# A kernel ordered by a planner: durations and port use in the list of steps corrected, and the first sums of w1 moved to the first part

## The chip, the cores and the metric

The kernel runs on one core of a Trainium2 chip. The metric is the device time of one execution in microseconds (us), median over several runs. The engines are named as in the profile: PE (TensorE, matmuls and transposes), ACT (ScalarE), DVE (VectorE), POOL (GpSimd) and SP (SyncE, which issues most of the transfers).

## The reference

Two blocks follow each other; all results are float32.

```
# block 1: attention with positive random features; q, k, v: (8, 8, 576, 64), omega: (128, 64)
x_s  = x / 64**0.25                                   # for q and k
h    = x_s @ omega.T - sum(x_s*x_s)/2
phi  = exp(h - max(h)) / sqrt(128)
kv   = phi(k).T @ v ;  z = sum over positions of phi(k)
x    = (phi(q) @ kv) / (phi(q) @ z + 1e-6)            # heads joined: (8, 576, 512)
# block 2: Fourier mixing and a multi-layer perceptron
u    = x + real(fft(fft(x, axis=1), axis=2))
un   = (u - mean(u)) / sqrt(var(u) + 1e-6)
out  = u + maximum(un @ w_ch1, 0) @ w_ch2             # w_ch1: (512, 2048), w_ch2: (2048, 512)
```

## The kernel before

**Two parts.** The first part works through 32 pairs of heads, 8 batches of 4 pairs. It also mixes each batch when its four pairs are there, converts both weight matrices from 64-bit to 32-bit floats, and puts the first four tiles of 128 rows ("plain" blocks) through the perceptron by plain products. The second part puts the other 4096 rows through it in eight blocks of 512 rows (`TB`), with products of half size in a Strassen-like scheme: sums of quarters of the weights and of the activations are formed on DVE and POOL, and fewer products are left for PE.

**A pair of heads** takes these steps (lines of the kernel before): transposes of k and q (`tps`, L396), evicted by ACT (`kqT`, L403); products with omega (`pp`, L471 for two heads at a time in quarters of the array, L461 for the odd column); maxima on DVE (`nmx`, L412) and exponentials on ACT (`e`, L424); the product with v (`kvp`, L506), kept by DVE or ACT (`kv`, L521 or L523); transposes of the query features (`tps`, L396); and the last products (`ndp`, L550 and L558), which DVE divides and writes to the batch's frame `x` (L571 to L581). L581 writes three times for each pair, and it is the pair's last step.

**Mixing a batch**: DVE, or for one half POOL, folds the frame (L608 to L636), PE multiplies by tables of cosines and sines (`yp`, L654; `ab`, L681 and L686), ACT and DVE combine the results (L700 to L708), and DVE and POOL add them to the frame (L716, L717), which SP stores to DRAM (`us`).

**Converting the weights**: 32 slabs of 128 x 512 numbers, 16 of w1 and 16 of w2, are loaded through POOL's queue (L358). For each slab, in the function `narrow`: L331 on POOL or L333 on ACT scales the upper words; L335, L337, L340 and L342 on DVE move bits; L344 on POOL adds. Only after all 32 slabs may `w2_parts` (L956) form sums of w2, which go to DRAM, and only then may the rows of the first block of the second part be normalised into the same slabs.

**A plain block**: normalised rows (L792 to L806) give `hp` (L863, 16 x 4 products), the relu `ht` is taken by ACT or DVE (L849, L847), and `op` (L886, 16 products of 512 columns) adds up the result, to which DVE adds the residual (L899).

**The second part**: `first_of` (products L1059, sums L1121 on POOL, relu sums L1047 on DVE, saves L1073 on ACT) and `product_of` (products L1204, sums L1174 on DVE, additions to the result L1243 on POOL or DVE). Before its first products, `weight_sums` forms four groups of sums of w1 on DVE (L1044): each group is four instructions of 128 x 512, for two of the eight columns of `first_of`. They lie in `w1s`, a buffer that is allocated when the buffers of the first part are freed, as `hid`, `hs` and the saves `s` are.

**What sets the order.** Every engine works through its instructions in the order in which they were issued. That order comes from a planner in the kernel (`Listing`): each stream yields steps (`Step`) with an engine or a choice of engines, a duration in us, what it waits for, what buffers it takes and gives, and a bias. The planner keeps a time at which each engine is free, and issues again and again the step that could start first, where the bias is added to the start for the comparison alone. The planned durations are thus not measured at run time; they only decide the order, and for steps with a choice the engine. `port=True` marks a step that uses the SBUF port which DVE and POOL share: the planner does not let two of these overlap. The central lines of its function `start`:

```
        if step.port:
            t = max(t, self.free[PORT])
        eng = min(step.engines, key=lambda e: max(t, self.free[e]) + step.engines[e])
```

Of the kernel before, what the change touches and what calls it, by code (L numbers as in the profile page):

```python
# [35 lines left out]
PORT = "port"  # L36
# [24 lines left out]

class Fork:
# [4 lines left out]
class Listing:  # L67
# [11 lines left out]
    def start(self, step, ready, before):  # L79
# [13 lines left out]
        if step.port:  # L93
            t = max(t, self.free[PORT])
        eng = min(step.engines, key=lambda e: max(t, self.free[e]) + step.engines[e])
        t = max(t, self.free[eng] if eng != NONE else 0.0)
        return t + (TURN if eng == PE and step.mode != self.mode else 0.0), eng

    def run(self, streams):
# [16 lines left out]
        while todo:  # L116
# [17 lines left out]
            if step.port:  # L134
                self.free[PORT] = end
# [46 lines left out]
def kernel(  # L182
# [38 lines left out]
    NWL, NSUM = 15, 3  # L221
# [37 lines left out]
    def loads():  # L259
        for n in range(B * NP):  # L260
# [7 lines left out]
            yield Step(SP, 0.45, 3.6, makes=("kq", n), kb=288)  # L268
            nc.sync.dma_start(kq[:, R : 2 * R, :], q[b, h].rearrange(rows, r=R))
            if n == 0:  # L270
                yield from load_v(0)

    def load_v(n):
        b, pr = divmod(n, NP)
        yield Step(SP, 0.6, 4.0, take=(f"vd{n % NV}",), makes=("vd", n), kb=288)
        nc.sync.dma_start(
            vds[n % NV][:, :, 0:D],
            v[b, 2 * pr : 2 * pr + 2].rearrange("i (p r) d -> (i p) r d", r=R),
        )

    def loads_v():
        for n in range(1, B * NP):
            yield from load_v(n)
# [25 lines left out]
    def load_tables():  # L309
        yield Step(NONE, after=(("kq", 2),))  # L310
        for n, a in tabs.items():
            yield Step(SP, 1.0, 4.0, makes=n, kb=a.nbytes / 1024)
# [8 lines left out]
    def narrow(i, dst, raw):  # L321
# [6 lines left out]
        step = Step({ACT: 0.7, POOL: 1.0}, after=(("raw", i),), bias=0.22)  # L328
# [5 lines left out]
        yield Step(DVE, 0.45, bias=0.02)  # L334
# [8 lines left out]
        yield Step(POOL, 1.3, makes=("w", i), give=("slab",), port=True, bias=0.12)  # L343
        nc.gpsimd.tensor_tensor(out=dst, in0=dst, in1=lof, op=ALU.add)  # L344

    def weights():
# [13 lines left out]
        yield Step(NONE, after=tuple(("w", i) for i in range(len(parts))), makes="converted", bias=1.84)  # L360
# [7 lines left out]
    def first():  # L368

        yield Step(NONE, 3.0, bias=-0.86)  # L370
# [29 lines left out]
    def evicted(dst, ps, j0, j1, makes, back):  # L400
        yield Step(ACT, 0.15 + 0.115 * (j1 - j0), 0.1, makes=makes + (j0,), give=("bank",), bias=0.03)
# [5 lines left out]
    def softmax(n, t, num, ps, es):  # L407
# [12 lines left out]
            ACT, 0.12 + 0.265 * num, 0.0, take=("e" if num == 4 else "e1",), give=("bank",), makes=("e", n, t), bias=0.17  # L420
# [11 lines left out]
    def attn(n):  # L432
# [16 lines left out]
        def pairs_of(js, *ts):  # L449
# [3 lines left out]
                0.45 if len(ts) == 1 else 1.0,  # L453
# [35 lines left out]
        def feature(c):  # L489
# [6 lines left out]
            1.35,  # L496
# [18 lines left out]
        def keep():  # L515
# [22 lines left out]
            1.3,  # L538
# [24 lines left out]
        yield Step(DVE, 1.6, after=(("frame", b),), give=("bank", "bank"), makes=("x", b, pr), bias=-0.06)  # L563
# [24 lines left out]
    def frames():  # L588
        for b in range(B):
            yield Step(NONE, take=(f"x{b % 2}",), makes=("frame", b), bias=0.16)  # L590


    def mix(b):
# [7 lines left out]
        def folds(n):  # L601
# [7 lines left out]
            step = Step({DVE: 1.15, POOL: 2.5} if n else DVE, 1.15, port=True)  # L609
            yield step  # L610
            eng = nc.gpsimd if step.eng == POOL else nc.vector
            eng.tensor_copy(
                out=h[:, NL, 0 : 2 * QD + 1 : 2 * QD], in_=x[:, 4, 0 : 2 * QD + 1 : 2 * QD]
            )
            for dst, src in ((h[:, 0:NL], h[:, 0:NL]), (h[:, NL : NL + 1], x[:, 4:5])):
                eng.tensor_tensor(
# [78 lines left out]
    def residual(b, c, x, ab):  # L695
        np_ = P if c < NL else 64
        yield Step(ACT, 0.4, 0.1, take=("bmp",), give=("bank",), bias=-0.02)
# [14 lines left out]
        def summed(g, left, right, which, dur):  # L712
            yield Step(which, dur, port=True, bias=-0.37)
# [6 lines left out]
            yield Step(SP, 0.4, 2.5, makes=("us", b, c, g), kb=2 * np_, bias=-1.96)  # L720
# [6 lines left out]
        yield Fork(summed(0, mi, pl, DVE, 0.8))  # L727
        if c < NL:
            yield from summed(1, pl, mi, POOL, 1.4)
        yield Step(NONE, after=(("us", b, c, 0),), give=("bmp",), bias=-1.98)  # L730
        if c == NL:
# [8 lines left out]
                kb=512,  # L740
# [42 lines left out]
    def norm_of(j, t, i, pool, dst):  # L783

        yield Step(SP, 0.5, 3.0, take=("u",), kb=256, bias=0.14)
# [5 lines left out]
        yield Step(DVE, 1.09, bias=0.16)  # L791
# [3 lines left out]
        yield Step(POOL, 0.6, port=True, bias=-0.1)  # L795
        nc.gpsimd.tensor_tensor(rstd[:], rstd[:], mhalf[:], op=ALU.pow)  # L796
        yield Step(DVE, 0.56, bias=-0.15)
# [7 lines left out]
        yield Step(ACT, 0.6, 0.1, give=("bank",), makes=("unT", j, i), bias=-0.27)  # L805
# [9 lines left out]
    def plain_norms():  # L815
        for j in range(NPLAIN):
            key = ("plain", j)
            yield Step(NONE, after=events_of([j]), take=("unT",), bias=0.34)
# [5 lines left out]
    def plain():  # L824
        for j in range(NPLAIN):
            if j == NPLAIN - 1:

                yield Step(NONE, after=(("x", B - 1, NP - 1),), bias=-0.24)
            yield from plain_of(j)

    def plain_of(j):
# [20 lines left out]
        for fc in range(NFC):  # L852
# [6 lines left out]
                give=("unT",) if fc == NFC - 1 else (), bias=0.19,  # L859
# [11 lines left out]
        for i in range(nt):  # L871
            for f0 in range(0, NFC, 2):
# [7 lines left out]
                    makes=("op", nt * j + i) if f0 == NFC - 2 else None, bias=0.18,  # L880
# [13 lines left out]
    def rest(t, yp):  # L894
        yield Step(SP, 0.5, 2.7, take=("ur",), kb=256, bias=1.91)
        ur = mlpp.tile([P, DM], F32, name="ur", tag="ur", bufs=1)
        load_rows(ur[:], t)
        yield Step(DVE, 0.7, after=(("op", t),), give=("bank",), bias=0.51)
# [38 lines left out]
    def w2_parts():  # L937
# [14 lines left out]
        def op(o, l, r, **kw):  # L952
            step = Step({DVE: 0.7, POOL: 1.35}, port=True, **kw, bias=0.39)
# [6 lines left out]
        for i, made_of in (  # L960
# [16 lines left out]
            yield Step(SP, 2.2, 4.5, after=(("w2t", i),), kb=7 * 256, makes=("w2l", i), bias=0.69)  # L977
# [7 lines left out]
        yield Step(NONE, after=last, give=("slab",) * 4, bias=1.32)  # L985
# [6 lines left out]
    def pairs(start):  # L992
# [11 lines left out]
        + [w2_parts(), block_norms(0, mlpp), plain(), weights()]  # L1004
# [16 lines left out]
    w1s = late.tile([128, 3, NDC // 2, DFF // 2], F32, name="w1s")  # L1021
    hid = late.tile([128, NFC, TB], F32, name="hid")
    hs = late.tile([128, HF, 3, HT], F32, name="hs")

    def sums_left(a11, a12, a21, a22, s1, s2, s4):

        return (
            (s1, a21, a22, ALU.add),
            (s2, s1, a11, ALU.subtract),
            (a21, a11, a21, ALU.subtract),  # L1030
            (s4, a12, s2, ALU.subtract),
        )

    def weight_sums():
        for g in range(4):
            f = slice(F2 // 4 * g, F2 // 4 * (g + 1))
            f2 = slice(F2 + f.start, F2 + f.stop)
            ops = sums_left(
# [298 lines left out]
```

## Time and profile before

| | us |
|---|---|
| median of 8 runs | 1237.85 (1237.3 to 1238.85) |
| the profiled execution, its own time | 1237.75 |
| its span from first to last instruction | 1236.0 |
| PE busy in the span | 1200.0 (97%) |
| DVE busy | 771.8 (62%) |
| ACT busy | 457.5 (37%) |
| POOL busy | 395.3 (32%) |
| first product of the second part starts at | 474.98 |

PE's busy time has modelled ends and includes products that run on a quarter of the array, so a busy PE isn't a PE at its peak. The granted clock of TensorE over the span is 0.996. In the groups of the profile the columns are: line, engine, operation, output and inputs with their shapes, count, then busy us, mean ns of one, and the idle time of the engine just before, with what ended it.

### The profile page before, as it was taken

Reading aid. Unit: us, or ns where it says so; the run is one execution under the profiler, and the core shown is the slowest. Engines: PE = TensorE matmul, PEld = TensorE weight load, DVE = VectorE, ACT = ScalarE, POOL = GpSimd, SP = SyncE. Lnnn points to the kernel's source line nnn. Section 1 sums busy time; section 2 is a strip of 40 time slices with the busy share of each in tenths; the row PEclk is TensorE's granted clock in tenths of the full one; section 3 lists DMA queues with packets and bytes.
Section 4 is the critical chain, followed back from the end, with each engine's and each line's share of the span. In section 5 each row is a group of like instructions: output and inputs, shape, how many; then the busy total and the mean of one; then the engine's idle time right before and its main releaser. Section 6 shows DMA issues by size and latency. Waiting matters only on the chain.

```text
span 1236.0 us, 31364 instructions
## 1 busy us (share of the span) xinstructions
PE 1200.0 (97%) x12513; PEld 1070.8 (87%) x12513; DVE 771.8 (62%) x1708; ACT 457.5 (37%) x1430; POOL 395.3 (32%) x462
## 2 busy tenths in 40 slices
PE   6999899999999998999999999999999999999997
PEld 5787778778887876899899899899899899899897
DVE  3999899997687525185185185186276276266265
ACT  5776666677664211222222222222222222222211
POOL 2544354643233110430430530530530530531430
PEclk8999999999999999999999999999999999999999
DMA  8655456646564345087078078078078068068155
GB/s 241 171 171 171 151 151 188 207 120 200 160 205 134 112 141 171 9 264 248 9 255 256 10 244 265 10 234 276 4 226 278 18 215 276 30 196 287 38 164 161
DMA packets 148737, 206.00 MB, mean 167 GB/s; under 512 B 49264, under 2 KB 62320, under 8 KB 148592
## 3 DMA queue, kind: packets, MB, share of 16 engines
q1 hardware_dynamic: 143984, 187.22, 48.2%
q0 software_dynamic: 4608, 16.78, 4.3%
q8 instruction: 100, 1.64, 0.5%
q14 instruction: 45, 0.37, 0.1%
HBM read 172.23 MB, written 35.91 MB: 168 GB/s over the span
## 4 chain that ended last, share of the span: by engine, by line
PE 83%; DVE 10%; ACT 3%; issue 2%; DMA 1%; SPq 0%; DVEq 0%; ACTq 0%
PE sx L1059 17%; PE sx L1204 16%; PE sz L1059 9%; PE sz L1204 8%; PE sy L1059 4%; PE hp L863 4%; PE sy L1204 4%; PE op L886 4%; PE tps L396 3%; PE yp L654 3%; PE pp L471 3%; ACT e L424 2%; DVE nmx L412 2%; PE kvp L506 1%; PE ndp L550 1%
## 5 line engine op out<-in xcount | busy, mean ns | idle before, releaser
L424 ACT ACTIVATE e<-pp,nmx 128x128 f32<-128x128 f32 x576 | 159.6, 407 | 47.2 <-DVE nmx L412 46.9
L1121 POOL TENSOR_TENSOR hs<-hid 128x256 f32<-128x256 f32 x64 | 46.6, 728 | 357.8 <-DVE hid L1047 330.2
L1047 DVE CUSTOM_DVE_ANT_0 hid<-sz,s 128x256 f32<-128x256 f32 x64 | 27.2, 425 | 182.4 <-PE sz L1059 174.4
L1059 PE MATMUL sx<-unT,w 128*128 128x256 f32 x512 | 127.7, 379 | 2.2 <-ACT s L1073 1.4
L1204 PE MATMUL sx<-wl,sums 128*128 128x128 f32 x896 | 115.4, 275 | 0.0
L1204 PE MATMUL sz<-wl,sums 128*128 128x128 f32 x896 | 114.2, 275 | 0.0
L412 DVE TENSOR_REDUCE nmx<-pp 128x4 f32<-128x512 f32 (+1 forms) x160 | 94.1, 628 | 31.1 <-PE pp L471 16.3
L1059 PEld LDWEIGHTS sx<-unT,w 128*128 128x128 f32 x512 | 96.6, 190 | 16.2 <-ACT s L1073 1.8
L1204 PEld LDWEIGHTS sz<-wl,sums 128*128 128x128 f32 x896 | 107.7, 192 | 0.4
L1204 PEld LDWEIGHTS sx<-wl,sums 128*128 128x128 f32 x896 | 107.6, 192 | 0.0
L1073 ACT ACTIVATE s<-sx 128x256 f32<-128x256 f32 x128 | 49.1, 384 | 152.1 <-PE sx L1059 74.2
L344 POOL TENSOR_TENSOR w<-w,raw 128x512 f32<-128x512 f32 x32 | 45.8, 1433 | 118.2 <-DVE raw L342 111.1
L1106 ACT ACTIVATE hid<-sx 128x256 f32<-128x256 f32 x64 | 24.6, 384 | 132.8 <-PE sx L1059 132.8
L471 PE MATMUL pp<-om,kqT 64*64 64x128 f32 x2048 | 71.1, 279 | 0.5 <-issue 0.3
L796 POOL TENSOR_TENSOR rstd<-rstd,mhalf 128x1 f32<-128x1 f32 x36 | 25.3, 704 | 142.8 <-DVE rstd L794 125.0
L471 PEld LDWEIGHTS pp<-om,kqT 64*64 64x64 f32 x2048 | 58.2, 136 | 11.9 <-issue 6.8
L1204 PE MATMUL sx<-wl,hid 128*128 128x128 f32 x512 | 67.6, 275 | 0.0
L863 PE MATMUL hp<-unT,w 128*128 128x128 f32 x512 | 62.2, 276 | 3.9 <-ACT e L424 2.9
L863 PEld LDWEIGHTS hp<-unT,w 128*128 128x128 f32 x512 | 59.5, 192 | 6.3 <-ACT e L424 3.5
L1059 PE MATMUL sx<-tt,w 128*128 128x256 f32 x256 | 64.2, 379 | 0.0
L1182 ACT ACTIVATE s<-sx 128x128 f32<-128x128 f32 x112 | 31.1, 278 | 88.5 <-PE sx L1204 60.7
L1059 PE MATMUL sz<-tt,w1s 128*128 128x256 f32 x256 | 61.9, 379 | 1.7 <-DVE w1s L1044 1.7
(134 smaller groups left out, 2578.6 us busy)
## 6 DMA issues: line engine op xcount, KB each, us to landing
wl<-w2l SPq DMA_DIRECT2D x392, 256.0 KB, 3.8
raw<-in_moe_w_ch_dram POOLq DMA_DIRECT2D x32, 512.0 KB, 4.8
kq<-in_k_dram SPq DMA_DIRECT2D x32, 288.0 KB, 3.6
kq<-in_q_dram SPq DMA_DIRECT2D x32, 288.0 KB, 5.0
vd<-in_v_dram SPq DMA_DIRECT2D x32, 288.0 KB, 4.7
out_dram<-ur SPq DMA_DIRECT2D x72, 128.0 KB, 3.0
u<-us SPq DMA_DIRECT2D x32, 256.0 KB, 4.5
ur<-us SPq DMA_DIRECT2D x32, 256.0 KB, 3.3
```

Of the source, the lines that this page charges most:

```text
L344: nc.gpsimd.tensor_tensor(out=dst, in0=dst, in1=lof, op=ALU.add)
L396: nc.tensor.transpose(ps[:, (j - j0) * 128 : (j - j0 + 1) * 128], src(j), ident[:])
L412: nc.vector.tensor_reduce(nmx[:, 0:num], ps[:, 0 : MF * num].rearrange("p (c m) -> p c m", m=MF), axis=AX.X, op=ALU.max, negate=True,)
L424: nc.scalar.activation(out=e[:, c, :], in_=ps[:, MF * c : MF * c + MF], func=AF.Exp, bias=nmx[:, c : c + 1],)
L471: nc.tensor.matmul(pps[c][cols, MF * m : MF * m + MF], lhsT=kqT[rows, j, cols], rhs=om2[rows, c, :],)
L654: nc.tensor.matmul(yp[:, 0:NK], lhsT=fold[:, c, n, :], rhs=tab[:, c, :], start=(c == 0), stop=(c == NC3 - 1),)
L863: nc.tensor.matmul(hp[:, 0:TP], lhsT=w1[:, dc, 128 * fc : 128 * fc + 128], rhs=unTs[key][:, dc, :], start=(dc == 0), stop=(dc == NDC - 1),)
L886: nc.tensor.matmul(yp[:, 0:DM], lhsT=hs[fc][:, 128 * i : 128 * i + 128], rhs=w2[:, fc, :], start=(fc == 0), stop=(fc == NFC - 1),)
L1059: nc.tensor.matmul(ps[:, 0:HT], lhsT=left(dc), rhs=right(dc), start=start and dc == 0, stop=(dc == D2 - 1), skip_group_check=True,)
L1073: nc.scalar.activation(out=s[:], in_=ps[:, 0:HT], func=AF.Copy)
L1121: nc.gpsimd.tensor_tensor(out=o, in0=l, in1=r, op=op)
L1204: nc.tensor.matmul(ps[:, 0:128], lhsT=left[:, f], rhs=wls[j, i, n][:, f], start=start and f == 0, stop=(f == 3), skip_group_check=True,)
```

## The change

These things are changed:

- The port is asked of the step and the engine: a step with `port=True` that goes to ACT no longer counts as using it, and one with a choice is planned with the port's time only for DVE and POOL.
- More steps are marked with `port`: L331 on POOL, L335, and the normalisation L798.
- Durations are set anew, as 1.4 instead of 1.0 us for L331 on POOL, 0.94 for `pp`, 1.1 for `kvp`, 1.23 for `ndp`, 0.85 and 1.6 for the sums L716 and L717; and many biases are set anew.
- The v of the first pair is a load of its own stream, no longer tied behind the first keys and queries; `kb` of a v load is set to 500.
- The second step of the second fold is always on DVE.
- The sums of the first of the four groups of w1 are made in the first part, after the last conversion, in a buffer `w1s0` of their own that lasts through both parts. The third sum of that group, which before overwrote a quarter of w1, goes to that buffer too, since plain blocks still read w1. `NWL`, the number of buffers for the loads of w2's parts, goes from 15 to 14.

```diff
+    def on_port(self, eng):
+        return self.port and eng in (DVE, POOL)
...
-        if step.port:
-            t = max(t, self.free[PORT])
-        eng = min(step.engines, key=lambda e: max(t, self.free[e]) + step.engines[e])
-        t = max(t, self.free[eng] if eng != NONE else 0.0)
+        def begin(e):
+            return max(t, self.free[e] if e != NONE else 0.0, self.free[PORT] if step.on_port(e) else 0.0)
+
+        eng = min(step.engines, key=lambda e: begin(e) + step.engines[e])
+        t = begin(eng)
...
-            if step.port:
+            if step.on_port(eng):
                 self.free[PORT] = end
...
-    NWL, NSUM = 15, 3
+    NWL, NSUM = 14, 3
...
             nc.sync.dma_start(kq[:, R : 2 * R, :], q[b, h].rearrange(rows, r=R))
-            if n == 0:
-                yield from load_v(0)
...
-        yield Step(SP, 0.6, 4.0, take=(f"vd{n % NV}",), makes=("vd", n), kb=288)
+        yield Step(SP, 0.6, 4.0, take=(f"vd{n % NV}",), makes=("vd", n), kb=500)
...
-            yield Step(SP, 1.0, 4.0, makes=n, kb=a.nbytes / 1024)
+            yield Step(SP, 1.0, 4.0, makes=n, kb=a.nbytes / 1024, bias=1.85)
...
-        step = Step({ACT: 0.7, POOL: 1.0}, after=(("raw", i),), bias=0.22)
+        step = Step({ACT: 0.72, POOL: 1.4}, after=(("raw", i),), port=True)
...
-        yield Step(DVE, 0.45, bias=0.02)
+        yield Step(DVE, 0.43, port=True)
         nc.vector.tensor_scalar(hi, hi, 0x80000000, None, op0=ALU.bitwise_and)
...
-        yield Step(ACT, 0.15 + 0.115 * (j1 - j0), 0.1, makes=makes + (j0,), give=("bank",), bias=0.03)
+        yield Step(ACT, 0.15 + 0.115 * (j1 - j0), 0.1, makes=makes + (j0,), give=("bank",), bias=-1.56)
...
-                0.45 if len(ts) == 1 else 1.0,
+                0.44 if len(ts) == 1 else 0.94,
...
-            1.35,
+            1.1,
             mode="quarters",
...
-            1.3,
+            1.23,
             mode="halves",
...
-            step = Step({DVE: 1.15, POOL: 2.5} if n else DVE, 1.15, port=True)
-            yield step
-            eng = nc.gpsimd if step.eng == POOL else nc.vector
-            eng.tensor_copy(
+            yield Step(DVE, 1.15, port=True)
+            nc.vector.tensor_copy(
...
-        yield Step(POOL, 0.6, port=True, bias=-0.1)
+        yield Step(POOL, 0.7, port=True, bias=0.23)
         nc.gpsimd.tensor_tensor(rstd[:], rstd[:], mhalf[:], op=ALU.pow)
-        yield Step(DVE, 0.56, bias=-0.15)
+        yield Step(DVE, 0.56, port=True)
...
+    GW = F2 // 4
+    w1s = [const.tile([128, 4, D2, GW], F32, name="w1s0")]
+
+    def weight_sums(groups):
+        yield Step(NONE, after=("converted",))
+        for g in groups:
...
+                if g == 0 and i == 2:
+                    o = w1s[0][:, 3]
+                nc.vector.tensor_tensor(out=o, in0=l, in1=r, op=op)
...
-        + [w2_parts(), block_norms(0, mlpp), plain(), weights()]
+        + [w2_parts(), weight_sums((0,)), block_norms(0, mlpp), plain(), weights()]
...
-    w1s = late.tile([128, 3, NDC // 2, DFF // 2], F32, name="w1s")
+    w1s += [late.tile([128, 3, D2, GW], F32, name=f"w1s{g}") for g in range(1, 4)]
...
-        product(x, lambda d: w1[:, d, f2], lambda d: un[1][:, d], False)
+        product(
+            x,
+            lambda d: w1s[0][:, 3, d, fg] if g == 0 else w1[:, d, f2],
+            lambda d: un[1][:, d],
+            False,
+        )
...
-    listing.run([late_norms(), halves(), loads_w2(), weight_sums()])
+    listing.run([late_norms(), halves(), loads_w2(), weight_sums((1, 2, 3))])
```

## The prediction

> **What bounds the kernel now.** I read the page first, then the busy time by stage, then the groups by form, then the timeline at two places. The page, parts 1 and 2:
>
> ```profile
> PE 1200.0 (97%) x12513; PEld 1070.8 (87%) x12513; DVE 771.8 (62%) x1708; ACT 457.5 (37%) x1430; POOL 395.3 (32%) x462
> PE   6999899999999998999999999999999999999997
> DVE  3999899997687525185185185186276276266265
> ```
>
> TensorE looks full throughout, but VectorE is full only in slices 2 to 9, and a PE that is "busy" on 64-wide products can be slow. The busy time by stage (columns: stretch, its length, then PE, PEld, DVE, ACT, POOL, each with its count, granted clock, DMA share, GB/s):
>
> ```profile
> 0.00:40.00 40.00, 29.66 (x604) 24.09 (x607) 19.46 (x40) 25.07 (x82) 12.39 (x23) 0.91 0.78 226
> 40.00:257.00 217.00, 205.06 (x3946) 172.01 (x3945) 206.56 (x490) 149.94 (x500) 103.80 (x94) 1.00 0.58 174
> 257.00:400.00 143.00, 140.01 (x2519) 118.05 (x2517) 112.79 (x295) 90.87 (x298) 44.08 (x38) 1.00 0.52 163
> 400.00:474.00 74.00, 74.00 (x417) 53.64 (x416) 30.60 (x72) 14.45 (x44) 8.01 (x10) 1.00 0.32 106
> 474.00:490.00 16.00, 12.10 (x54) 9.91 (x54) 11.86 (x20) 3.30 (x9) 0.34 (x1) 1.00 0.77 257
> 490.00:584.00 94.00, 94.00 (x633) 88.12 (x633) 49.78 (x102) 22.46 (x64) 29.28 (x39) 1.00 0.56 179
> ```
>
> From 40 to 257 us DVE is 95% busy (206.56 of 217) and sets the pace; from 257 on DVE has gaps and PE sets it; a block of the second part (490 to 584) is PE at 94.0 of 94.0. So time can come only from 0 to 490.
>
> What DVE does in its full stage, from the groups by form (columns: count, busy us, mean ns, idle before):
>
> ```profile
> L335 DVE TENSOR_SCALAR raw<-raw 128x512 uint32<-128x512 uint32 x32 | 21.8, 699 | 0.0
> L337 DVE SCALAR_TENSOR_TENSOR w<-w,raw 128x512 uint32<-128x512 uint32 x32 | 27.6, 863 | 0.3
> L340 DVE TENSOR_SCALAR raw<-w 128x512 uint32<-128x512 uint32 x32 | 19.8, 620 | 1.1
> L331 POOL TENSOR_SCALAR w<-raw 128x512 f32<-128x512 f32 x27 | 44.9, 1670 | 27.0 <-DMA raw<-in_moe_w_ch_dram 26.8
> L333 ACT ACTIVATE w<-raw 128x512 f32<-128x512 f32 x5 | 3.6, 711 | 1.1 <-DMA raw<-in_moe_w_ch_dram 1.1
> ```
>
> The view of line 335 alone gives the spread, min/median/max:
>
> ```profile
> L335 DVE TENSOR_SCALAR raw<-raw x32: 409/421/1584, 30.0 to 264.7; 128x512 uint32<-128x512 uint32 x32
> ```
>
> Half of these take 421 ns, some up to 1584: the excess is about the length of a POOL instruction. The same views give medians 682 for L337 and 430 for L340. A conversion thus loses (699-421)+(863-682)+(620-430) = 0.65 us of DVE to collisions with POOL.
>
> Two places of the timeline fix the clock of the argument. The twentieth of the 32 attention pairs ends here (L581 writes its result), and the second part begins so:
>
> ```profile
> 255.53 0.94 DVE L581 TENSOR_TENSOR x<-ndp,rden 128x256 f32<-128x256 f32 x3
> 474.98 1.96 PE L1059 MATMUL sx<-unT,w 128*128 128x256 f32 x8 [0.87 <-DVE ur L899]
> 477.82 0.69 DVE L1044 TENSOR_TENSOR w1s<-w 128x512 f32<-128x512 f32 x1 [2.98 <-DMA out_dram<-ur]
> 478.61 1.97 PE L1059 MATMUL sz<-tt,w1s 128*128 128x256 f32 x8 [1.67 <-DVE w1s L1044]
> ```
>
> **The change, part by part.** The list decides order and engine, so I compared the instruction orders of both programs, which are fixed when they are built.
>
> *To the twentieth pair.* At the lowest duration of each group, the DVE rows up to there add to 230.0 us before and 229.3 after: no work leaves DVE. What can leave is the collisions. Through pair 20 the old list has 28 conversions: 28 x 0.65 = 18.2 us; with the small copies L612 (8 x 0.17), the sums L716 and L717 (8 x 0.20 and 8 x 0.30 over their lowest) and L608 and L798 (0.5), 24 us. In the new order line 331 runs 15 times on POOL (26 before, through that pair) and the rest on ACT. If collisions go with that count, 42% of 24 go: 10 us. All of them at most: 24. L331, L335 and L798 are now kept off the port by the list, which before counted none of the three, so more than the count should go. I take 15, nearer to the end that a count supports; the lower bound is 0, if real times drift from the planned ones. Pair 20 then ends at 256.5-15 = 241.5.
>
> A rule that speaks against this: by the Trainium skill, GPSIMD Engine Reference, Engine selection, a one-input operation runs on GpSimd at roughly line rate; its elementwise section has 1.03 cycles per element, an estimated 0.44 us for 512, so moving 11 of them would free 4.8 us of port and the gain would be nearly nil. The row says 1670 ns, so I go by 11 x 1.67 = 18 us of freed port time. The skill also says (SBUF — State Buffer, Who interferes with whom) that the loser of the pair blocks fully and issue order decides which it is; by that some waits would only move to POOL, which no row here prices apart.
>
> *From there to the second part.* PE prices, from start-to-start distances where it does not wait: a transpose 0.115, sixteen pp products 1.03 and the whole one 0.54, kvp 1.10, ndp 1.32, hp 0.223 and op 0.859 each, yp 0.54 each, an ab group 1.3. The first part is 425.8 us of PE work. Before: 213.6 are done at pair 20 and 212.2 remain, which took 475.0-256.5 = 218.5, so PE lost 6.3. After: 208.4 are done, 217.4 remain. The mix differs: 175.5 of them lie before the end of pair 32 (132.7 before) and only 41.9 behind it (79.5), since three of the four plain blocks are now threaded between pairs. The loss falls where work is interleaved (400 to 474 is full), so 6.3 x 175.5/132.7 = 8.3. DVE has 369.5-229.3 = 140 us of work in that stretch, under PE's 175, so PE sets it. First part: 241.5+217.4+8.3 = 467.2, that is 7.8 earlier.
>
> *The change of parts.* The first sums of w1 (4 x 0.69 us of DVE) move ahead of pair 21, under DVE's 30 idle us of 257 to 400; without that cover, +2.8. Their buffer no longer lies in space that the last store frees, so the 1.67 us wait at 478.61 goes. The sixteen sums kept DVE until 487.96, and PE then waited 1.36 for an ACT save whose buffer DVE still read; with twelve left, interleaved with the relu sums, most of that goes. What is late next is that ACT save, at 477.96 behind the same store. I take -2.5, bounds 0 and -3.
>
> *Edits at nothing.* ACT gets 12 conversions and 9 ht and loses 20 kv copies: 8.5+2.5-5.2 = +5.8 us, under its 67 idle us of 40 to 257. DVE gets those copies, three more w2 sums and one fold more, all inside the sums above. SP: keys and queries of the second pair go ahead of the first v. PE waited 4.45 us for those keys, so -0.5, and v lands later by two 288 KB transfers, 2.4 us at 240 GB/s, against 3.7 us of room before 20.8. Table loads sn, cd and sd go behind two pairs of loads, 7 us of 30. Fourteen wl buffers: loads run 14 x 0.89 = 12.5 us ahead of use and land in 3.8. Seven ur sums move from POOL to DVE in the second part, 4.8 us over eight blocks in which DVE is 53% busy.
>
> Sum: -7.8-2.5-0.5 = -10.8. The profiled execution took 1237.75 (span 1236.0 and 1.75 around it), 0.1 under the median; 1237.85-10.8 = 1227.
>
> **Rivals.** *Slower: PE starves between the pairs.* PE takes its list in order; plain blocks threaded between pairs stop the pairs behind them whenever weights or ht are late. At the prices above PE lost 24 of 217 us in 40 to 257, 11%; the old stretch from pair 20 to 32 lost little, but had PE and DVE less tightly packed. With 11% lost there: 175.5/0.89 = 197.2 in place of 183.8, and if only 5 us of collisions go: 10 more. -10.8+13.4+10 = +12.6, 1250. For: both engines are packed denser there than before. Against: the new list prices pp, kvp and ndp near their rows. It decides from 10.8 us of loss more than I count. *Collisions only move.* Change = 4.2 minus what is saved of the 24; nothing saved gives 1242, and 4.2 saved gives no change. For: the spread of L335 shows that start times decide. Against: 11 fewer POOL instructions of 1.67 us. *More goes.* 24 saved and no extra loss: -22, 1216. *The new list orders the first part no better:* then only the change of parts counts, 1235; its chance lies inside the two before.
>
> **How the numbers follow.** Forecast, 8 to 20 us of collisions saved, 1222 to 1234: 0.50. More goes, down to 1212: 0.18. Collisions only move, 1235 to 1242: 0.17. PE starves, 1240 to 1258: 0.15. Faster by over 0.2% (2.5 us, about what a measurement of this kernel can tell from no change) is 0.50+0.18 and a little of the third: 0.70. Same 0.09, slower 0.21. The range leaves out a tail of the second and of the fourth: 1212 to 1246. The forecast's own range is 1222 to 1234.
>
> **What would show it.** Right: L335's mean falls from 699 to near 520, pair 20 ends near 241, the second part starts near 467, and the wait of sz on w1s is gone. Wrong: pair 20 near 256 with the same means (collisions moved), or pair 20 early but the second part at 475 or later with hp or op waiting in the list of waits (starved PE), or PE waits within a block of the second part, where I count none.

## The result, and the profile after

The changed kernel takes 1242.82 us (median of 12 runs, 1239.11 to 1244.8) against 1237.47 for the kernel before on the same chip: ratio 1.0041, interval 1.0033 to 1.0049. It is slower by 5.4 us, where 10.8 us less was predicted; its profiled execution took 1244.28. Most lines of the kernel after stand 2 to 17 further down in its file: L335, L337 and L340 of before are now L339, L341 and L344, and the scaling on POOL and ACT, L331 and L333, is now L335 and L337.

The page of the kernel after, parts 1 and 2:

```profile
PE 1203.7 (97%) x12513; PEld 1073.0 (86%) x12513; DVE 768.2 (62%) x1732; ACT 465.2 (37%) x1431; POOL 358.2 (29%) x437
PE   7899999999999999999999999999999999999997
DVE  3989888996576765285185186276276276266265
```

POOL lost 37 us of work, DVE 3.6. DVE's row has eights in slices 3, 6 and 7, where before it had nines. The busy time by stage (columns as before the change):

```profile
0.00:40.00 40.00, 28.48 (x617) 23.57 (x617) 17.38 (x38) 25.34 (x83) 11.15 (x22) 0.96 0.76 213
40.00:257.00 217.00, 202.78 (x3743) 170.13 (x3745) 195.78 (x492) 146.96 (x467) 83.42 (x84) 0.98 0.56 169
257.00:400.00 143.00, 140.72 (x2220) 115.57 (x2213) 97.42 (x247) 83.37 (x270) 28.16 (x26) 1.00 0.54 167
400.00:474.00 74.00, 74.00 (x888) 57.60 (x887) 49.71 (x137) 31.98 (x103) 13.47 (x16) 1.00 0.35 119
474.00:490.00 16.00, 15.13 (x59) 10.30 (x58) 9.16 (x15) 2.58 (x7) 0.00 (x0) 1.00 0.43 127
490.00:584.00 94.00, 93.58 (x631) 87.71 (x630) 52.37 (x107) 22.84 (x65) 28.22 (x37) 1.00 0.60 193
```

In the stage of 40 to 257 us DVE does 10.8 us less (195.78 against 206.56), but PE does 2.3 us less too (202.78 against 205.06). The block of the second part now has 0.42 us in which PE waits. The groups of the conversion and the view of one line:

```profile
L339 DVE TENSOR_SCALAR raw<-raw 128x512 uint32<-128x512 uint32 x32 | 16.8, 546 | 0.3 <-POOL w L335 0.3
L341 DVE SCALAR_TENSOR_TENSOR w<-w,raw 128x512 uint32<-128x512 uint32 x32 | 26.3, 822 | 0.3
L344 DVE TENSOR_SCALAR raw<-w 128x512 uint32<-128x512 uint32 x32 | 15.9, 498 | 1.1
L335 POOL TENSOR_SCALAR w<-raw 128x512 f32<-128x512 f32 x15 | 23.6, 1586 | 12.8 <-DMA raw<-in_moe_w_ch_dram 12.7
L339 DVE TENSOR_SCALAR raw<-raw x32: 410/422/1534, 29.4 to 277.6; 128x512 uint32<-128x512 uint32 x32
```

The collisions did fall: over the same medians a conversion loses 0.33 us now, 0.65 before. But the pair that was to end at 241.5 and the second part that was to begin at 467.2 stand here in the timeline:

```profile
257.40 0.95 DVE L585 TENSOR_TENSOR x<-ndp,rden 128x256 f32<-128x256 f32 x3
481.12 1.96 PE L1071 MATMUL sx<-unT,w 128*128 128x256 f32 x8 [0.87 <-DVE ur L901]
482.92 1.89 PE L1071 MATMUL sz<-tt,w1s 128*128 128x256 f32 x8
```

Pair 20 ends 1.9 us later than before, the second part begins 6.14 later (481.12 against 474.98), and the wait of `sz` on `w1s` is gone. PE's waits, by what ended them (us in total, times, longest):

```profile
PE kvp L510 <- ACT e L428: 6.0, 9, 2.6
PE sz L1221 <- ACT s L1199: 2.9, 7, 0.4
PE kvp L510 <- DMA vd<-in_v_dram: 2.2, 1, 2.2
```

The first was 1.2 us before, the other two are new. In the profiled execution PE stands idle 28.89 us up to the second part (26.13 before) and is busy for 452.23 (448.85 before): 2.76+3.38 = 6.14. It runs at half its clock for 13.65 us of that stretch (6.83 before). Half of the added time, 3.41, is as much as the busy time grew, but that the clock made it grow isn't shown: in the list alone (a run below), with only 3.41 us at half clock, less than before, the busy time is 451.08, still 2.2 more. The granted clock over a whole execution varies from run to run, and its mean over after's executions (0.995) is that of before in the later comparisons, so the clock doesn't separate the medians.

The second part can be priced from the starts of its blocks. The new numbers of its norms cost 3.6 us: with the old ones back (a run below) the first block is 0.43 us shorter, and six blocks take 94.0 us instead of 94.52. The change of parts gains 3.3: the first block takes 93.44 us in that run, 96.72 before. As an estimate that mixes medians and profiles, 5.4 = 3.6 - 3.3 + 5.1, and the 5.1 is left for the first part.

### The profile page after: what moved, and what is told of

Same layout as the page of the kernel before. It is cut to its first block, busy times and chain, and to the rows that moved or that the text cites. A ratio compares the mean times of both kernels' runs of the same rounds, so it can differ in the third digit from the quotient of the medians.

```text
span 1242.4 us, 31332 instructions
## 1 busy us (share of the span) xinstructions
PE 1203.7 (97%) x12513; PEld 1073.0 (86%) x12513; DVE 768.2 (62%) x1732; ACT 465.2 (37%) x1431; POOL 358.2 (29%) x437
## 4 chain that ended last, share of the span: by engine, by line
PE 87%; DVE 7%; ACT 3%; issue 1%; DMA 1%; POOL 0%; SPq 0%; DVEq 0%; ACTq 0%
PE sx L1071 18%; PE sx L1221 16%; PE sz L1071 9%; PE sz L1221 8%; PE sy L1071 4%; PE hp L865 4%; PE sy L1221 4%; PE op L888 4%; PE tps L400 4%; PE yp L656 4%; PE pp L475 3%; ACT e L428 2%; PE kvp L510 2%; PE ab L683 2%; PE ndp L554 2%; PE tp L804 1%
## 5 line engine op out<-in xcount | busy, mean ns | idle before, releaser
L1071 PE MATMUL sx<-unT,w 128*128 128x256 f32 x448 | 111.1, 379 | 0.9 <-DVE ur L901 0.9
L1071 PEld LDWEIGHTS sx<-unT,w 128*128 128x128 f32 x448 | 84.5, 190 | 12.8 <-issue 1.7
L798 POOL TENSOR_TENSOR rstd<-rstd,mhalf 128x1 f32<-128x1 f32 x36 | 20.0, 556 | 151.5 <-DVE rstd L796 140.3
L1071 PE MATMUL sx<-tt,w1s 128*128 128x256 f32 x256 | 63.2, 380 | 0.0
L1071 PE MATMUL sz<-unT,w1s 128*128 128x256 f32 x256 | 63.1, 379 | 0.0
L1071 PE MATMUL sy<-unT,w 128*128 128x256 f32 x256 | 63.1, 379 | 0.0
```

Source lines behind the costliest of these rows:

```text
L1071: nc.tensor.matmul(ps[:, 0:HT], lhsT=left(dc), rhs=right(dc), start=start and dc == 0, stop=(dc == D2 - 1), skip_group_check=True,)
```

## The experiments

Four accounts of the loss were held against each other: the edits besides the list cost it; DVE's time was not on the path and the order got worse, for what the new numbers say; the order got worse because before's list had been fitted so closely that any other order loses; the clock of PE, which fell to half more often, took it. All ratios are to the kernel before, run on the same chip in the same comparison; differences in us are between the medians of that comparison. "First product" is the start of the second part's first product in the profiled execution.

**The parts of the change alone.** *The list alone* (after, but `w1s` and its sums as before and 15 `wl` buffers):

```diff
-        + [w2_parts(), weight_sums((0,)), block_norms(0, mlpp), plain(), weights()]
+        + [w2_parts(), block_norms(0, mlpp), plain(), weights()]
-    listing.run([late_norms(), halves(), loads_w2(), weight_sums((1, 2, 3))])
+    listing.run([late_norms(), halves(), loads_w2(), weight_sums()])
```

> Only the list of the change (durations, biases, port); w1's sums and the 15 buffers as before. In the profile of the changed kernel the second part starts 6.1 us later (481.1 for 475.0), the change of parts wins about 3 us, and seven waits of 0.41 us in the second part lose 2.9. If the list is the cause of the late start: the second part starts near 481 again, the waits of 1.67 and 1.36 us at its start are back, about 1243 to 1246. If moving the sums of w1 upset the order of the first part instead: start near 475, 1236 to 1239.

Measured 1248.37 us, 1.0096 (1.0082 to 1.011). First product at 481.56, two waits of 1.91 and 1.36 us at the change of parts, blocks of 94.52. So the list costs 11.4 us, and more than all of the loss is in it.

*The buffers alone* (`NWL, NSUM = 14, 3` in before):

> The kernel before with 14 instead of 15 buffers for the parts of w2; the order of PE, DVE, ACT and POOL is unchanged, only loads move in SP's order. If the seven waits of 0.41 us in the changed kernel's second part come from the missing buffer: 2.9 us slower, 1240.4. If they come from the other order of that part: no change, within 0.5 us of before.

1236.17 us, 0.9998 (0.9988 to 1.0007): nothing, as counted.

*The sums of w1 alone* (before's list, the change's edits to `w1s` and its sums, 14 buffers):

```diff
-        + [w2_parts(), block_norms(0, mlpp), plain(), weights()]
+        + [w2_parts(), weight_sums((0,)), block_norms(0, mlpp), plain(), weights()]
-    listing.run([late_norms(), halves(), loads_w2(), weight_sums()])
+    listing.run([late_norms(), halves(), loads_w2(), weight_sums((1, 2, 3))])
```

> The kernel before with the first sums of w1 in the first part and 14 buffers, the old list. If the list is the cause of the loss: the first part stays near 475 and the 1.67 and 1.36 us waits at the change of parts go, 2.5 to 3 us faster, 1234.5 to 1235. If moving the sums upsets the order: 1238 or more.

1244.58 us, 1.006 (1.0045 to 1.0075). The first part's last product ended at 471.17, but the second part began only at 480.72. The timeline of this run shows why, with the residual L899 issued ahead of the last sums of w2, and SP's queue (SPq) standing until PE makes the transposes of the norms (L802):

```profile
443.18 0.69 DVE L899 TENSOR_TENSOR ur<-ur,op 128x512 f32<-128x512 f32 x1 [6.35 <-PE op L886]
446.92 0.69 DVE L956 TENSOR_TENSOR sums<-big,sums 128x512 f32<-128x512 f32 x1
449.39 22.57 SPq L772 DMA_DIRECT2D u<-us  x3
471.00 1.04 PE L802 MATMUL tp<-ident,u 128*128 128x128 f32 x8
```

DVE waits for PE at L899, and the sums of w2 behind it end at 447.6 (431.8 before). Of the three loads of rows for the second part's first norms, two go at once; the third stands in SP's queue from 451.2 to 471.6, since the two buffers `u` come free only with the transposes at 471.00, which this order puts behind the last 32 products `op`. Before, those transposes stood at 455.78 and 464.49. It is the place in the order that costs this, as the next run shows.

*The sums of w1 after those of w2*, one line off the run before:

```diff
     def weight_sums(groups):
-        yield Step(NONE, after=("converted",))
+        yield Step(NONE, after=("converted", ("w2l", 7)))
```

> Before with the first sums of w1 made in the first part, in the listing after the last sums of w2, and 14 buffers for wl; the old list. If only the place of these sums in the order spoilt the run that had them after the conversions, PE goes from the first part to the second without the three waits of before (3.0 us) and without a gap: 1233 to 1235. If eight more operations of DVE near the end of the first part hold its last norms up anyway, a gap of 3 to 10 us stays before the second part: 1237 to 1244.

1233.52 us, 0.9967 (0.9953 to 0.998). In its profile PE has no wait from the second part's first product (478.12) to 490: the 3 us at the change of parts are real.

**What DVE's time is worth.** *Half the masks left out*, in before's order:

```diff
-        nc.vector.tensor_scalar(hi, hi, 0x80000000, None, op0=ALU.bitwise_and)
+        if i % 2 == 0:
+            nc.vector.tensor_scalar(hi, hi, 0x80000000, None, op0=ALU.bitwise_and)
```

> The order of before, with the sign mask (L335, 699 ns in the mean of before) left out in 16 of 32 weight slabs, so that half of the converted weights are wrong: some 11 us less work on DVE between 40 and 257 us, and nothing else changed. If DVE sets the pace there, as the prediction had it, the first part ends 7 to 11 us earlier and the time is 1226 to 1230. If DVE and PE bind in turn and the shared port's waits were slack in this order, the first part ends 0 to 3 us earlier and the time is 1234 to 1237.

1233.47 us, 0.9973 (0.9964 to 0.9983). The groups of this run, one line lower from L336 on:

```profile
L336 DVE TENSOR_SCALAR raw<-raw 128x512 uint32<-128x512 uint32 x16 | 9.6, 600 | 0.0
L338 DVE SCALAR_TENSOR_TENSOR w<-w,raw 128x512 uint32<-128x512 uint32 x32 | 25.5, 798 | 0.1
L341 DVE TENSOR_SCALAR raw<-w 128x512 uint32<-128x512 uint32 x32 | 21.6, 676 | 1.1
```

In these lines DVE is spared (21.8-9.6)+(27.6-25.5)-(21.6-19.8) = 12.5 us; over the whole span its busy time falls by 8.8 (771.8 to 763.0), since other lines wait longer. The median gains 3.5: 0.28 of the one, 0.4 of the other. DVE was 95% busy and still did not set the pace alone.

*15 more conversions issued on ACT*, in before's order, so that ACT has 19 and POOL 13:

```diff
-        if step.eng == POOL:
+        if step.eng == POOL and i not in (4, 5, 7, 8, 13, 17, 19, 20, 22, 23, 25, 26, 27, 28, 29):
```

> Before's order with 15 more of the 32 weight conversions issued on ACT (L333, 704 ns) and taken from POOL (L331, 1670 ns), nothing else changed. If DVE's waits for the shared port are on the path, as the prediction had it, DVE's work between 40 and 257 us falls and the first part ends 6 to 10 us earlier: 1228 to 1232. If only about a third of what DVE is spared reaches the end, as with the mask left out, 2 to 4 us earlier: 1234 to 1236. If ACT's queue, which also makes e, then holds PE up, it ends 0 to 5 us later: 1237 to 1243.

1234.54 us, 0.9982 (0.9972 to 0.9992). Its groups:

```profile
L331 POOL TENSOR_SCALAR w<-raw 128x512 f32<-128x512 f32 x13 | 22.4, 1726 | 21.5 <-DMA raw<-in_moe_w_ch_dram 21.4
L335 DVE TENSOR_SCALAR raw<-raw 128x512 uint32<-128x512 uint32 x32 | 20.5, 660 | 0.0
L337 DVE SCALAR_TENSOR_TENSOR w<-w,raw 128x512 uint32<-128x512 uint32 x32 | 25.8, 807 | 0.3
```

POOL's L331 is halved (44.9 to 22.4 us), but the conversion's collisions fall only from 0.65 to 0.54 us (L340 has a mean of 606 ns here). They do not go with the count of L331. The trace of before shows beside what the long instances of the three DVE lines lie: of some 21 us of excess, 13 lie beside POOL's additions L344, which no kernel here takes from POOL, and under 6 beside L331. One such pair:

```profile
44.25 1.27 POOL L344 TENSOR_TENSOR w<-w,raw 128x512 f32<-128x512 f32 x1 [1.70 <-DVE raw L342]
44.34 1.47 DVE L335 TENSOR_SCALAR raw<-raw 128x512 uint32<-128x512 uint32 x1
```

ACT's queue takes 19 conversions without a loss.

**The clock.** PE's two half-clock stretches that begin at 52.58 and 189.12 us in after come behind waits of 1.39 and 2.57 us; here PE is kept running ahead of them by transposes of the identity into PSUM columns that nothing reads:

```diff
+            if n == 4 and ts[0] == 3:
+                for _ in range(13):
+                    nc.tensor.transpose(pps[0][:, 0:128], ident[:], ident[:])
...
+        if n == 15:
+            for _ in range(19):
+                nc.tensor.transpose(kvp[0][:, 128:256], ident[:], ident[:])
```

> The changed kernel with 13 transposes of the identity ahead of the pp step of pair 5 that waited 1.39 us, and 19 ahead of the kvp step of pair 16 that waited 2.57 us, into columns that nothing reads; no step is taken from its place. The changed kernel's clock was 0.5 from 52.6 to 59.4 and from 189.1 to 192.5 us. Theory clock: the halved clock after these waits is the loss; it stays at 1.0, and up to 3.4+1.7 = 5.1 us come back, 1238 to 1240. Theory chain: PE waits for a chain of DVE and ACT and the clock only rides on it; the time stays within 1 us of 1242.8, or grows by the 1.4 to 2 us of added work.

1248.23 us, 1.0092 (1.0072 to 1.0112). In its profile no half clock is left before the end, and the second part begins at 479.49, 1.6 us earlier than in after but still 4.5 later than before. The list alone, with less half clock than before (3.41 against 6.83 us), starts its second part as late as after. So the clock is at most a small part of what was lost there. Its other executions are slower than after's and ran at a lower mean clock (0.990 to 0.994, after's 0.995), so their median doesn't test the clock; why they did, and what the added transposes cost in them, stays open.

**Which of the list's numbers.** *Durations and port without the biases*, in before's list:

```diff
-        step = Step({ACT: 0.7, POOL: 1.0}, after=(("raw", i),), bias=0.22)
+        step = Step({ACT: 0.72, POOL: 1.4}, after=(("raw", i),), bias=0.22, port=True)
-        yield Step(DVE, 0.45, bias=0.02)
+        yield Step(DVE, 0.43, bias=0.02, port=True)
...
```

> Before with the new durations, the new port marks and the new rule of the port, its old biases kept. If the durations themselves order the first part worse, the first part ends at 478 to 483 and the blocks of the second part may lengthen to 94.5: 1242 to 1249. If the loss comes from the new biases, the first part ends at 472 to 476: 1235 to 1239. If any change of the numbers shifts the order off a fitted set, both this and its counterpart are 5 to 11 us slower.

1255.52 us, 1.0153 (1.0134 to 1.0172), first product at 491.36. *The biases without those:*

```diff
-        step = Step({ACT: 0.7, POOL: 1.0}, after=(("raw", i),), bias=0.22)
+        step = Step({ACT: 0.7, POOL: 1.0}, after=(("raw", i),))
-        yield Step(POOL, 0.6, port=True, bias=-0.1)
+        yield Step(POOL, 0.6, port=True, bias=0.23)
...
```

> Before with the new biases alone, its old durations and port marks kept. If the biases carry the loss: 1242 to 1249, and this is the whole of it. If the durations carry it: 1235 to 1239. If any change of the numbers shifts the order off a fitted set, this one is 5 to 11 us slower too, and the losses of the two don't add up to that of the list as a whole (11 us).

1251.57 us, 1.012 (1.0101 to 1.0138), first product at 489.2, but blocks of 93.87. Each of the two loses more than the whole list (18.6 and 14.6 against 11.4), so the new biases take back part of what the durations and the port cost (the new loads of v and the second fold are in neither). That looked like a list fitted so closely that any other order loses. Three kernels tested it, each with one number of before moved by 0.02 us.

```diff
-            ... makes=("e", n, t), bias=0.17
+            ... makes=("e", n, t), bias=0.15
```

> Before with one bias moved by 0.02 us (ACT's e, 0.17 to 0.15), which says nothing of the chip but sorts the first part another way. If before's list is one that was fitted to its result, so that another order, whatever its reason, loses as a rule, this is 4 to 12 us slower: 1241 to 1249. If the loss of the list lies in what its numbers say, this is 1235 to 1239.

```diff
-        yield Step(DVE, 0.45, bias=0.02)
+        yield Step(DVE, 0.43, bias=0.02)
```

> Before with one duration moved by 0.02 us (the sign mask of DVE, 0.45 to 0.43, which is the new list's number), nothing else. Fitted list: 1241 to 1249. Loss in what the numbers say: 1235 to 1239, since 0.02 us in a step of 0.43 says next to nothing.

```diff
-        yield Fork(summed(0, mi, pl, DVE, 0.8))
+        yield Fork(summed(0, mi, pl, DVE, 0.82))
```

> Before with one duration moved by 0.02 us (DVE's sums of windows, 0.8 to 0.82, toward the new list's 0.85), nothing else. Fitted list: 1241 to 1249. Loss in what the numbers say: 1235 to 1239.

1237.29 (0.9998, 0.9988 to 1.0007), 1232.27 (0.9953, 0.9938 to 0.9968) and 1238.45 us (1.0015, 1.0003 to 1.0027). The theory that any other order loses falls: reshuffles that mean nothing gave +0.3, -4.7 and +1.5 us. A weaker form of it stands, since three moves of one number can't test it: that dozens of numbers were fitted to each other, and any part of a list loses without the rest. The new biases, alone and with the old marks, lost 14.6. The second of the three moves, the new list's own 0.43 for the mask, gains more than either theory expected, and its stage of 40 to 257 us shows how, PE at 208.76 with DVE as full as before:

```profile
40.00:257.00 217.00, 208.76 (x4031) 177.85 (x4030) 206.84 (x495) 156.01 (x517) 95.11 (x87) 1.00 0.57 174
```

Two more runs ask which numbers lose. *The port's count alone* (rule and marks in before's list) and *the durations alone*:

```diff
+        def begin(e):
+            return max(t, ..., self.free[PORT] if step.on_port(e) else 0.0)
...
-        step = Step({ACT: 0.7, POOL: 1.0}, after=(("raw", i),), bias=0.22)
+        step = Step({ACT: 0.7, POOL: 1.0}, after=(("raw", i),), bias=0.22, port=True)
-        yield Step(DVE, 0.45, bias=0.02)
+        yield Step(DVE, 0.45, bias=0.02, port=True)
-        yield Step(DVE, 0.56, bias=-0.15)
+        yield Step(DVE, 0.56, bias=-0.15, port=True)
```

> Before with the shared port counted as the new list counts it (the rule, and the marks on the conversions of ACT and POOL, the sign mask and the norm's scaling), its old durations and biases. Three meaningless moves of 0.02 us gave between -5 and +1.5 us, so an effect of over 4 us to the slow side is one of the numbers. If counting the port spoils the order (the list keeps DVE and PE's partners apart for waits that were slack): 1243 to 1256, most of the 18.6 us of durations and port together. If the durations do: 1232 to 1240 here.

```diff
-        step = Step({ACT: 0.7, POOL: 1.0}, after=(("raw", i),), bias=0.22)
+        step = Step({ACT: 0.72, POOL: 1.4}, after=(("raw", i),), bias=0.22)
-        yield Fork(summed(0, mi, pl, DVE, 0.8))
+        yield Fork(summed(0, mi, pl, DVE, 0.85))
...
```

> Before with the new durations alone (conversions 0.72 and 1.4, mask 0.43, y and sums of the windows, norm's power), without the new marks and rule of the port and with the old biases. If the durations spoil the order against the biases that were kept: 1243 to 1256. If counting the port does: 1232 to 1240 here. If the two only lose together, both are at 1232 to 1240.

The port's count alone: 1256.14 us, 1.0161 (1.0143 to 1.0179). The durations alone: 1241.85, 1.0047 (1.003 to 1.0065), which is 6.3 us, as much as the meaningless moves spread (6.2), though none of those lost more than 1.5. The port's count alone loses most of all parts tried, 20.6 us. Its executions ran at a mean clock of 0.992, those of before beside them at 0.996: an estimated 4 us of the 20.6 go with that. Groups of the run with it, and a row of its waits (lines 5 further down than in before):

```profile
L340 DVE TENSOR_SCALAR raw<-raw 128x512 uint32<-128x512 uint32 x32 | 15.3, 478 | 0.0
L342 DVE SCALAR_TENSOR_TENSOR w<-w,raw 128x512 uint32<-128x512 uint32 x32 | 36.6, 1144 | 0.9
L345 DVE TENSOR_SCALAR raw<-w 128x512 uint32<-128x512 uint32 x32 | 15.8, 493 | 1.1
PE sz L1209 <- ACT s L1187: 9.2, 7, 1.3
```

The mask now hardly meets POOL (478 ns, 699 before), but the instruction behind it meets it instead (1144, 863 before): (478-421)+(1144-682)+(493-430) = 0.58 us for a conversion against 0.65. The plan that keeps one instruction off the port runs the next into it: 14 of the 15 long instances of L342 lie beside POOL's addition. And PE waits 1.3 us in each block of the second part: 95.42 us for a block, 10 of the 20.6 us in seven of them.

**The second part.** *norm_of's new numbers in before's list:*

```diff
-        yield Step(POOL, 0.6, port=True, bias=-0.1)
+        yield Step(POOL, 0.7, port=True, bias=0.23)
-        yield Step(DVE, 0.56, bias=-0.15)
+        yield Step(DVE, 0.56, port=True)
...
```

> Before with the new numbers of norm_of alone (durations, biases and port marks of the norms and their transposes). The first part shares little of it (its norms come at its end), so it should end within 2 us of 474. If these numbers are what puts ACT's s behind PE in the second part, the blocks take 94.52 us instead of 94.0 and the time is 1239 to 1242; if something else of the list does, the blocks stay at 94.0 and the time is 1236 to 1238.

1244.54 us, 1.0061 (1.0045 to 1.0078): blocks of 94.52, and the same row of waits, "PE sz L1204 <- ACT s L1182: 2.9, 7, 0.4". First product at 477.51, 8.5 us after the last one of the first part, so the norms are late there as well; I had expected that part to keep its time. *The other way round*, after with norm_of's old numbers in the second part:

```diff
+        old = pool is not mlpp
-        yield Step(DVE, 0.56, port=True)
+        yield Step(DVE, 0.56, port=not old, bias=-0.15 if old else 0.0)
...
```

> After, with norm_of's old numbers in the second part alone; its first part is after's. If norm_of's new numbers are all of the second part's loss, its blocks take 94.0 us again, the first part ends at 478 to 482 as in after, and the time is 1237.5 to 1240.5. If the second part's loss has another source in the list, the blocks stay at 94.52 and the time at 1241 to 1244.

1239.01 us, 1.0024 (1.0007 to 1.0041), against 1.0041 for after; blocks of 94.0 again, which is 3.6 us of the second part. The mechanism stands in the timeline of after at the end of a block (PE's next block starts at 669.51):

```profile
662.80 0.60 ACT L808 ACTIVATE unT<-tp 128x512 f32<-128x512 f32 x1 [1.05 <-PE tp L804]
663.43 0.69 DVE L933 TENSOR_TENSOR tt<-unT,unT 128x512 f32<-128x512 f32 x1 [0.16 <-ACT unT L808]
665.48 0.28 ACT L1199 ACTIVATE s<-sz 128x128 f32<-128x128 f32 x1 [2.08 <-DVE unT L933]
666.75 1.13 PE L1221 MATMUL sz<-wl,sums 128*128 128x128 f32 x8 [0.42 <-ACT s L1199]
```

The last norm of the block comes 6.7 us before its end, the four sums that it releases take DVE, ACT's save waits for DVE, and PE for ACT. Before, that last norm stood 18.6 us ahead of the end of its block:

```profile
647.14 0.60 ACT L806 ACTIVATE unT<-tp 128x512 f32<-128x512 f32 x1 [0.87 <-PE tp L802]
```

A step marked for the port starts late in the plan whenever the port is taken, and unmarked steps go ahead of it; with the port's count alone the norm is as late as in after (6.7 us before the end), with the old numbers back it is 18.6 us ahead again. The mark doesn't do this in every list: with the new durations beside it (the run of durations and port) the norm stands 17.0 us ahead and a block takes 94.14 us.

**A faster kernel.** The sums of w1 after w2's, with norm_of's new biases alone in the second part:

```diff
+        new = pool is not mlpp
-        yield Step(POOL, 0.6, port=True, bias=-0.1)
+        yield Step(POOL, 0.6, port=True, bias=0.23 if new else -0.1)
...
```

> The kernel with w1's sums after w2's, and norm_of's new biases (not its new durations or port mark) in the second part alone. With the blocks at 93.87 us, as in the run with the new biases alone, the second part is 0.9 us shorter than with 94.0: 1232 to 1234.5 if the sums of w1 give their 3 us, 0.9 us below the kernel beside it in any case. If the shorter blocks came from the first part's order, they take 94.0 or 94.5 and the time is that of the kernel beside it or up to 4 us more.

1232.32 us, 0.996 (0.9947 to 0.9973), blocks of 93.87. With the 15 conversions on ACT besides, by the same line as above:

> The fastest kernel so far (w1's sums after w2's, norm_of's new biases in the second part), with the 15 weight conversions more on ACT and off POOL that gave 1.8 us in before's order. If the two add up: 1229.5 to 1231.5. If the gain of the conversions was that of another chip's run, 1231.5 to 1233.5.

1230.49 us, 0.9937 (0.992 to 0.9953), faster than both kernels:

```profile
474.00:490.00 16.00, 16.00 (x75) 14.01 (x75) 10.61 (x20) 3.51 (x10) 4.02 (x6) 1.00 0.85 295
```

PE has no wait from 474 to 490. The mask's 0.43, which gained 4.7 us in before's order, was not tried together with these.

## Why the prediction was wrong

**The step that failed first is "To the twentieth pair": "I take 15 ... Pair 20 then ends at 256.5-15 = 241.5."** It ended at 258.35. Two things were wrong in it. The size: the collisions of the 28 conversions that it counts fell by 28 x 0.32 = 9 us, and the stage's DVE work by 10.8, near the 10 that a count of L331 gave, not 15. That the count came near is partly luck, since most of the excess lies beside POOL's additions. The price, which matters more: I took each microsecond of DVE for one of the path, since "DVE is 95% busy and sets the pace". With the masks left out it was worth 0.28 to 0.4. Ten us saved are then some 3 to 4.

By the prediction's own prices PE had lost 42.9 us at the end of pair 20 before (256.5-213.6) and had lost 50.0 in after (258.35-208.4), with 5.2 us less work done. So all that the first part lost in this execution was lost where 15 us were to be gained.

**The sum had no term for the order itself.** The step treats the two orders up to pair 20 as the same work in the same time and moves only collisions. The runs put the new list at +11.4 us, of which some 3.6 lie in the blocks and most of the rest in the first part. Busy time by stage shows it in two places; the first two rows are the kernel before, the last two the kernel after:

```profile
60.00:80.00 20.00, 19.83 (x383) 17.09 (x385) 19.69 (x47) 13.73 (x46) 7.50 (x9) 1.00 0.40 125
150.00:190.00 40.00, 37.97 (x736) 32.03 (x734) 39.52 (x86) 26.52 (x91) 22.23 (x18) 1.00 0.49 148
60.00:80.00 20.00, 20.00 (x321) 16.74 (x314) 15.08 (x43) 12.91 (x40) 6.03 (x7) 1.00 0.36 106
150.00:190.00 40.00, 34.16 (x659) 27.70 (x652) 35.63 (x80) 25.19 (x81) 16.71 (x15) 0.99 0.48 146
```

Before, PE and DVE are full together. After, DVE has gaps of 4.9 and 4.4 us in the stretches shown: from 60 to 80 us PE has work that gives DVE none (`yp` and `ndp`, while DVE waits 4.3 us for pp), and from 150 to 190 both wait for each other along pp, maxima, e and kvp (the wait of kvp on e grew from 1.2 to 6.0 us over the run). With the old biases the port's count is the costliest part, as the run that has it alone shows. That it is also what loses the first part's time in the whole list is not shown: with the count alone DVE has 19.80 and 38.24 us of work in these two stretches, so its losses lie elsewhere, and the biases alone lose too. Why the plan spreads PE's and DVE's work worse stays open; that a marked step sinks behind unmarked ones, as the norm of the second part does, is argued only.

**"PE waits within a block of the second part, where I count none"** was the second failed step, named there as what would make it wrong: +3.6 us, from norm_of's numbers, shown from both sides. I had looked at the second part for its sums and not for the order of its norms.

**The rival "PE starves between the pairs"** had the sign, but its place was wrong. From pair 20 on, at the prediction's own prices, PE lost 481.12-258.35-217.4 = 5.4 us (6.3 before, 8.3 foretold), so threading the plain blocks between the pairs did no harm there. "Collisions only move" holds for the port's count alone, not for the whole list, in which the collisions halved.

**Right:** the change of parts, -2.5 foretold; the two waits (3.0 us) are gone, and the first block is 3.3 us shorter with the old norms. The 14 buffers at nothing. **Half right:** SP's loads. The keys' wait fell by 4.7 us (5.7 to 1.0), but v's room of 3.7 us did not hold: kvp waited 2.2 for it, and PE's idle time to 40 us rose by 1.2.

The Trainium skill (GPSIMD Engine Reference, Engine selection) says that one-input operations run on GpSimd at roughly line rate. The rows don't agree, with means of 1586 to 1726 ns for L331 on POOL against 698 to 752 on ACT (before, after, and the run with 15 more on ACT). By that rule the gain of moving them would have been nearly nil, and the 1.8 us that the run with 15 more of them on ACT gained come near it for other reasons: most of DVE's excess lies beside POOL's additions, and DVE's time had a low price.

## What to carry to other kernels

An engine that is 95% busy is not the bound if the one it feeds is as full: price its time by taking some of it away in the unchanged order, before a sum is built on it. A change of a planner's numbers is above all another order; here three meaningless moves of 0.02 us spread over 6.2 us, so an estimate of one needs a term of that size, and a result inside it is no verdict on the numbers. Counting a shared resource as exclusive can cost more than the collisions, as it did here with the old biases: steps that others wait for can sink in the order, and the next instruction can run into what the first was spared. Before such a count, look beside which instructions the long instances lie.

## What the runs showed of the hardware

The same DVE instruction on 128 x 512 numbers (L335) takes 421 ns in the median and up to 1584 beside POOL's work. DVE's waits for POOL are not in proportion to POOL's instructions: with half of L331 gone, 5/6 of them stayed. The half-clock stretches of PE, apart from the one at the end, last 3.41 us or a multiple of it, and come behind waits as short as 1.39 us (at 52.58 in after, where PE was busy for 1.83 of the 3.48 us ahead); among ten executions of one kernel (after with the old norms) the time went from 1235.1 at a mean clock of 0.997 to 1244.5 at 0.989.
